# A recurrence with a feed-forward on one core: SyncE's issues in the list, later moves and stores, kept banks, later feed-forward ranks

## The chip, the core and the metric

The kernel runs on one core of a Trainium2 chip. The metric is the device time of one execution in microseconds; several runs are taken and their median is given. A core has five engines, each with its own instruction queue that is worked off in order: TensorE (PE, with its weight loads PEld), VectorE (DVE), ScalarE (ACT), GpSimd (POOL) and SyncE (SP). They wait for each other by semaphores. Transfers are issued by SyncE and by GpSimd here and are carried by 16 DMA engines. TensorE writes into PSUM, which has eight banks.

## The reference

For 4 batches with 8 heads, 768 time steps and a head size of 40, a state of 40 x 40 per head is carried through time. Its outputs, gathered to 3072 tokens of 320, go through a feed-forward with squared ReLU:

```python
for t in range(S):                         # S = 768, per batch and head
    y[t]  = rt @ state
    Sa    = state @ at
    state = state * wt[None, :] - outer(Sa, bt) + outer(vt, kt)
x = y as (3072, 320)
h = x @ w_in                               # 320 x 2048
g = maximum(h, 0) ** 2
out = g @ w_out                            # 2048 x 320
```

## The kernel before

**The work.** Time is cut into 6 chunks (c) of 128 steps. A chunk has 4 input batches of 8 heads, so there are 24 units m = 4 c + batch, and each unit has two steps of 4 heads: 48 steps st = 2 m and 2 m + 1. A unit has

- six loads `("L", m, key)` of 160 KB for W, K, B, A, V, R (L244, issued on SyncE). Each of the six has a ring of four buffers, so a load of unit m can start only when unit m - 4 has been read;
- its preparation: logarithm and running sum of W (L257, L263), exponentials (L268), products KB (L279), casts on GpSimd (L285, L290), and transposes (L294) with their copies out of PSUM.

Each step is then a chain through PE, ACT and DVE: `ca` (L394), masked copies `CN` (L402), `P`, `corr1`, `corr2` (L417, L426), `tb` (L463), `ex` (L482), `EVX` (L487), `kbm` (L498), and at its end the outputs `YS` (L511) and the state `UZ` (L515). Four steps later in the list than `ca`, these close the step. From step 12 on, `ca` of one step and `ex` of the step three before are merged into one piece of PE work that takes four PSUM banks at once.

**The feed-forward.** Four steps (half a chunk, h = 0 to 11) give 256 tokens. Two of the eight heads lie on rows where the matmul cannot use them, so four small SBUF-to-SBUF transfers `("mv", h, x)` (L620, SyncE) move them first. Then come eight pieces `hp` (L630, six matmuls each into one bank), ReLU `hs` on ACT (L636), the square `Gt` on GpSimd or DVE (L641); then for two token blocks `op` (L658, sixteen matmuls in two parts), the copy `osb` (L662, ring of three) and the store `st` (L667, SyncE). Banks held by the feed-forward are capped at four, those of the preparation at three.

**The weights.** `w_in` comes as ten transfers into WIN[0..2], `w_out` as one into WOUT. GpSimd issues them (L596, L602), and the transfer makes bf16 of them.

**The order.** All of it is first collected as operations (`op(name, engine, rank, cost, lat, needs, bufs, fn)`): `cost` is how long the engine is taken, `lat` when the result is there, both in us, and the rank is about the step at which the operation is due. `listed()` then plays the engines forward. For each engine it looks at the first 60 open operations in the order of rank, works out by `beginning()` when each could start (engine free, needs ended, buffers and banks free), takes those within 0.06 us of the earliest, and of these the one with the lowest rank. The operations are emitted in that order. So the plan decides the order in each queue, and the chip keeps that order, whatever the real durations are: an operation whose input comes later than the plan thought holds up all that is behind it on its engine.

In the plan before, loads are on an engine of their own, "DQ", that stands for the DMA engines (0.97 us each). Moves and stores are on "SP" at 0.1 and 0.3 us. On the chip, loads, moves and stores are issued by SyncE's one queue, in the order of their planned starts. The weights take a time on "DQ" first (`WINq`, `WOUTq`), and the real issue on GpSimd is planned behind that.

Of the kernel before, what the change touches and what calls it, by code (L numbers as in the profile page):

```python
# [18 lines left out]
def kernel(  # L19
# [12 lines left out]
    nc = tc.nc  # L32

    NB, NHH, T, D = r.shape
    L = 128
# [11 lines left out]
    NH = 2 * NCH  # L47
# [68 lines left out]
    def act(n, more=0.0):  # L116
        return 0.093 + 0.00083 * n + more, 0.186 + 0.00083 * n

    def pe(n):
        return n, n + 0.165  # L120
# [20 lines left out]
    WIN = [gl.tile([128, DFF], BF16, name=f"WIN{g}") for g in range(PB - 1)]  # L141
    WOUT = gl.tile([128, NJ, DM], BF16, name="WOUT")
# [75 lines left out]
    for m in range(NBC):  # L218
        o = Batch()
# [18 lines left out]
    def add_load(m, key, rank):  # L238
        o = bt[m]
        c, bb = divmod(m, NB)  # L240

        def go():
            t_ = sb(o.nat[key], [128, NHH, D], FP32)
            nc.sync.dma_start(  # L244
                out=t_[:],
                in_=nat_srcs[key][bb, :, c * L:(c + 1) * L, :].rearrange("h t e -> t h e"))
        op(("L", m, key), "DQ", rank, 0.97, 3.0, [], [o.nat[key]], go)

    def add_prep(m):
        o = bt[m]  # L250
# [317 lines left out]
    def add_energy(hc):  # L568
        st0 = hc * (NQ // 2)
        c, q = divmod(st0, NQ)  # L570
        for x, (src, at) in enumerate(((Mcb[c], AM), (Ccb[c], AC))):
            jmb[hc, x] = buf("jm")

            def jm(x=x, src=src, at=at):
# [11 lines left out]
    MOVED = [(s, 64 * x + D, 2 * NG + s, (64 - D) * x, n)  # L586
             for s in range(2) for x, n in enumerate((64 - D, 2 * D - 64))]

    def add_weights():
        for g in range(NG):  # L590
            def go(g=g):
                if g == 2:
                    nc.vector.memset(WIN[2][:], 0.0)
                for p, row, h, e0, n in PLACE + MOVED:
                    if p == g:
                        nc.gpsimd.dma_start(out=WIN[p][row:row + n, :],  # L596
                                            in_=moe_w_in[h * D + e0:h * D + e0 + n, :])
            op(("WINq", g), "DQ", g - 4.0, 2.8, 2.8, [], [], lambda: None)
            op(("WIN", g), "POOL", g - 4.0, 0.3, 1.0, [("WINq", g)], [], go)

        def go():
            nc.gpsimd.dma_start(out=WOUT[:], in_=moe_w_out.rearrange("(j p) f -> p j f", p=128))  # L602
        op(("WOUTq",), "DQ", -1.5, 8.3, 8.3, [], [], lambda: None)
        op(("WOUT",), "POOL", -1.5, 0.5, 1.0, [("WOUTq",)], [], go)

    Gtb = [buf("Gt") for _ in range(NH)]

    def add_ff(h):
        c, hf = divmod(h, 2)
        st0 = c * NQ + hf * (NQ // 2)  # L610
        done = [("YS", st0 + i) for i in range(NQ // 2)]
        X_ = YSb[c]

        def by_pair():
            return X_.tile[:].rearrange("e (b p) t -> e p b t", b=NB)[:, :, HB * hf:HB * hf + HB, :]

        for x, (p, row, hh, e0, n) in enumerate(MOVED):
            def gather(p=p, row=row, hh=hh, e0=e0, n=n):
                src = 64 * (hh % 2) + e0
                nc.sync.dma_start(out=by_pair()[row:row + n, p], in_=by_pair()[src:src + n, hh // 2])  # L620
            op(("mv", h, x), "SP", st0 + 7.3 + 0.01 * x, 0.1, 2.0, done, [X_], gather)
        for jj in range(NJ // 2):
            hpb, hsb = buf("bank", "ff"), buf("hs")

            def ff_in(jj=jj, hpb=hpb):
                hp = hpb.tile[:].rearrange("p (u a b) -> p u a b", u=2, a=HB)
                for u in range(2):
                    j = 2 * jj + u
                    for g in range(NG):
                        nc.tensor.matmul(out=hp[:, u], lhsT=WIN[g][0:ROWS[g], j * 128:(j + 1) * 128],  # L630
                                         rhs=by_pair()[0:ROWS[g], g],
                                         start=(g == 0 and u == 0), stop=(g == NG - 1),
                                         skip_group_check=True)

            def relu(hpb=hpb, hsb=hsb):
                nc.scalar.activation(out=sb(hsb, [128, 512], BF16)[:], in_=hpb.tile[:],  # L636
                                     func=ACTF.Relu)

            def square(jj=jj, hsb=hsb, eng=None):
                t_ = sb(Gtb[h], [128, NJ, HB, L], BF16)  # L640
                eng.tensor_tensor(out=t_[:, 2 * jj:2 * jj + 2].rearrange("p j a b -> p (j a b)"),  # L641
                                  in0=hsb.tile[:], in1=hsb.tile[:], op=ALU.mult)

            rank = st0 + 8.0 + 0.45 * jj
            on = "POOL" if jj % 4 and h < NH - 1 else "DVE"
            op(("hp", h, jj), "PE", rank, *pe(0.654),
               [("mv", h, x) for x in range(len(MOVED))] + [("WIN", g) for g in range(NG)],
               [X_, hpb], ff_in, "F")
            op(("hs", h, jj), "ACT", rank + 0.3, *act(500), [("hp", h, jj)], [hpb, hsb], relu)
            op(("Gt", h, jj), on, rank + 0.6, *((0.99, 1.05) if on == "POOL" else (0.34, 0.45)),  # L650
               [("hs", h, jj)], [hsb, Gtb[h]],
               lambda f=square, on=on: f(eng=nc.gpsimd if on == "POOL" else nc.vector))
        for b_ in range(HB):
            opb, osbb = buf("bank", "ff"), buf("osb")

            def ff_out(part_, b_=b_, opb=opb):
                for j in range(part_ * NJ // 2, (part_ + 1) * NJ // 2):
                    nc.tensor.matmul(out=opb.tile[:, 0:DM], lhsT=Gtb[h].tile[:, j, b_, :],  # L658
                                     rhs=WOUT[:, j, :], start=(j == 0), stop=(j == NJ - 1))

            def copy_out(opb=opb, osbb=osbb):
                nc.scalar.activation(out=sb(osbb, [128, DM], FP32)[:], in_=opb.tile[:, 0:DM],  # L662
                                     func=ACTF.Copy)

            def store(b_=b_, osbb=osbb):
                tok = (HB * hf + b_) * T + c * L
                nc.sync.dma_start(out=out[tok:tok + L, :], in_=osbb.tile[:])  # L667

            for p in range(2):
                op(("op", h, b_, p), "PE", st0 + 10.8 + 1.8 * b_ + 0.3 * p, *pe(1.085),  # L670
                   [("Gt", h, 4 * p + i) for i in range(4)] + [("WOUT",)]
                   + ([("op", h, b_, 0)] if p else []),
                   [Gtb[h], opb], lambda p=p, f=ff_out: f(p), "F")
            op(("osb", h, b_), "ACT", st0 + 11.5 + 1.8 * b_, *act(302), [("op", h, b_, 1)],
               [opb, osbb], copy_out)
            op(("st", h, b_), "SP", st0 + 11.6 + 1.8 * b_, 0.3, 2.0, [("osb", h, b_)], [osbb], store)

    for m in range(NBC):
        add_prep(m)
# [19 lines left out]
    def add_guard():  # L699
# [6 lines left out]
        def judge():  # L706
# [21 lines left out]
    CROSS = {("PE", "ACT"): 0.05, ("PE", "DVE"): 0.05, ("ACT", "PE"): 0.11, ("DVE", "PE"): 0.11,  # L728
             ("ACT", "DVE"): 0.06, ("DVE", "ACT"): 0.06, ("POOL", "PE"): 0.11, ("SP", "PE"): 0.1}
    SWITCH, SLACK = 0.095, 0.06  # L730
    BIAS = {"FR": 0.3, "FC": 0.6, "CR": 0.3}
    START = {"PE": 4.0, "ACT": 2.2, "DVE": 4.0, "POOL": 5.2, "SP": 0.9, "DQ": 0.9}

    def listed():
        free = dict(START)
# [11 lines left out]
        out_ = []  # L747
        seen = set()

        def beginning(o, e):  # L750
            t = free[e]
            for nm in o.needs:
                d = ops[alias.get(nm, nm)]
                if d.end is None:
                    return None
                t = max(t, d.end + (CROSS.get((d.eng, e), 0.17 if e == "POOL" else 0.08)
                                    if d.eng != e else 0.0))
            new = 0
            for b_ in o.bufs:
                if b_.slot is not None:  # L760
                    continue
                if b_.ring == "bank":
                    new += 1
                    if b_.kind and held.get(b_.kind, 0) + 1 > CAP[b_.kind]:
                        return None
                else:
                    n = RING[b_.ring if b_.ring in RING else "N"]
                    if heads[b_.ring] != b_.n:
                        return None
                    if b_.n >= n:  # L770
                        old = rings[b_.ring][b_.n - n]
                        if old.left:
                            return None
                        t = max(t, old.end + 0.1)
            if new:
                spare = sorted(freed[i] for i in range(NBANK) if i not in taken)
                if len(spare) < new:
                    return None
                t = max(t, spare[new - 1] + 0.1)
            return t  # L780

        while any(todo.values()):
            best = None
            for e, row in todo.items():
                cand = []
                for o in row[:60]:
                    t = beginning(o, e)
                    if t is not None:
                        cand.append((t, o))
                if not cand:  # L790
# [153 lines left out]
```

## Time and profile before

| | us |
|---|---|
| median of 3 runs | 336.72 (335.22 to 338.42) |
| the profiled execution | 337.33 |
| its span, first to last instruction | 335.6 |
| mean granted TensorE clock | 0.92 |

The profile is of one execution. Busy times count instructions that compute; register, semaphore and DMA-issuing instructions are not counted, except in rows named SPq. A row of a wait names the waiting line, then what released it. Matmuls are pipelined and their ends are modelled, so that a busy PE need not be PE at its peak. Line numbers are those of the kernel before.

### The profile page before, as it was taken

How to read it: one execution, taken by the hardware profiler on the slowest of the kernel's cores; microseconds unless marked ns; L12 is line 12 of the kernel's file. 1: busy time of each engine (PE TensorE's matmuls, PEld its weight loads, DVE VectorE, ACT ScalarE, POOL GpSimd, SP SyncE). 2: the span in 40 equal slices, each digit the busy share in tenths (PEclk: the TensorE clock that was granted, in tenths of full speed). 3: DMA queues.
4: the chain of work that ended last, by engine and by line, in shares of the span. 5: the costliest groups of instructions: out<-in, count | busy, mean ns of one | idle time of the engine just before them, and what ended most of it. 6: DMA issues, size and time to landing. Idle time of an engine off the chain costs nothing.

```text
span 335.6 us, 9943 instructions
## 1 busy us (share of the span) xinstructions
PE 286.5 (85%) x3852; PEld 221.8 (66%) x3852; DVE 228.9 (68%) x523; ACT 203.7 (61%) x531; POOL 205.0 (61%) x350
## 2 busy tenths in 40 slices
PE   6798675578999599899699699899899898998894
PEld 4565454357778377687488587688687776776562
DVE  6579947046888669697478668697688688684330
ACT  4655444158896476776477477777687675656241
POOL 8658527157998569297378468396685682555300
PEclk9559959599999879999899979999999999799978
DMA  8996296439999698699725744633000001001011
GB/s 137 176 157 121 36 168 92 66 66 163 191 161 176 124 190 136 129 178 177 136 52 88 144 76 81 123 61 62 26 2 25 24 2 38 10 2 46 5 44 48
DMA packets 158472, 31.37 MB, mean 93 GB/s; under 512 B 152976, under 2 KB 158096, under 8 KB 158416
## 3 DMA queue, kind: packets, MB, share of 16 engines
q1 hardware_dynamic: 155808, 28.03, 46.5%
q0 software_dynamic: 2608, 2.62, 5.1%
q8 instruction: 32, 0.52, 0.7%
q14 instruction: 24, 0.20, 0.2%
HBM read 28.84 MB, written 3.93 MB: 98 GB/s over the span
## 4 chain that ended last, share of the span: by engine, by line
PE 51%; DMA 15%; DVE 14%; SPq 7%; POOL 4%; issue 4%; ACT 4%; DVEq 0%; POOLq 0%; ACTq 0%
PE bank L630 18%; PE bank L658 10%; DMA YS<-YS 7%; SPq L620 6%; PE bank L294 6%; DVE EVX L487 4%; PE bank L498 4%; DVE CN L402 3%; DMA WOUT<-in_moe_w_out_dram 3%; PE bank L263 3%; PE bank L394 2%; DMA NW<-in_w_dram 2%; PE bank L426 2%; DMA NA<-in_a_dram 2%; POOL KB L279 2%
## 5 line engine op out<-in xcount | busy, mean ns | idle before, releaser
L630 PE MATMUL bank<-YS,WIN 120*128 120x256 bf16 (+1 forms) x576 | 86.4, 294 | 24.7 <-DMA YS<-YS 24.1
L641 POOL TENSOR_TENSOR Gt<-hs 128x512 bf16<-128x512 bf16 x66 | 68.5, 1041 | 32.3 <-ACT hs L636 32.0
L636 ACT ACTIVATE hs<-bank 128x512 bf16<-128x512 f32 x96 | 57.0, 598 | 50.7 <-PE bank L630 44.8
L630 PEld LDWEIGHTS <-WIN 120*128 120x128 bf16 (+1 forms) x576 | 56.1, 104 | 43.4 <-DMA YS<-YS 24.7
L487 DVE TENSOR_TENSOR EVX<-bank,MEX 128x512 bf16<-128x512 f32 x96 | 65.1, 684 | 14.0 <-PE bank L482 12.8
L402 DVE TENSOR_TENSOR CN<-bank,MCN 128x512 bf16<-128x512 f32 x96 | 64.6, 682 | 4.2 <-PE bank L394 3.7
L658 PE MATMUL bank<-WOUT,Gt 128*128 128x320 bf16 x384 | 60.1, 302 | 7.1 <-DMA WOUT<-in_moe_w_out_dram 7.1
L658 PEld LDWEIGHTS <-Gt 128*128 128x128 bf16 x384 | 35.6, 98 | 20.1 <-issue 7.1
L451 ACT ACTIVATE jk<-CN 128x512 bf16<-128x512 bf16 x48 | 30.1, 628 | 16.5 <-DVE CN L402 16.3
L443 POOL TENSOR_TENSOR x<-Mc,c 128x160 f32<-128x160 bf16 x48 | 23.5, 490 | 26.5 <-DVE c L439 26.1
L515 DVE TENSOR_TENSOR UZ<-bank,GT 64x80 bf16<-64x80 f32 x80 | 18.8, 236 | 25.6 <-PE bank L505 13.4
L279 POOL TENSOR_TENSOR KB<-NK,GI 128x320 bf16<-128x320 f32 (+1 forms) x25 | 21.2, 850 | 24.1 <-ACT GI L268 23.8
L641 DVE TENSOR_TENSOR Gt<-hs 128x512 bf16<-128x512 bf16 x30 | 15.1, 503 | 23.5 <-ACT hs L636 23.3
L342 ACT ACTIVATE KBT<-bank 128x1024 bf16<-128x1024 bf16 (+1 forms) x25 | 24.7, 987 | 9.7 <-PE bank L294 7.8
L447 POOL TENSOR_TENSOR Cc<-x,EVX 128x160 bf16<-128x160 f32 x48 | 23.8, 496 | 9.9 <-ACT EVX L536 8.5
L426 PEld LDWEIGHTS <-CN 128*128 128x128 bf16 x384 | 21.2, 99 | 8.9 <-issue 4.0
L439 DVE TENSOR_TENSOR c<-bank,Mc 128x160 bf16<-128x160 f32 x48 | 15.3, 319 | 16.9 <-PE bank L426 15.1
L498 PE MATMUL bank<-EVX,KB 128*64 128x168 bf16 x384 | 24.7, 248 | 1.7 <-DVE EVX L487 1.5
L474 DVE COPY TB<-bank 128x512 bf16<-128x512 bf16 (+1 forms) x48 | 18.9, 395 | 4.6 <-PE bank L469 3.8
L263 PE MATMUL bank<-lnW,UTI 128*128 128x320 f32 x48 | 21.0, 523 | 1.2 <-ACT lnW L257 0.9
L511 DVE TENSOR_TENSOR YS<-bank,GT 128x256 bf16<-128x256 f32 x48 | 20.2, 421 | 2.5 <-PE bank L505 2.1
L268 ACT ACTIVATE GI<-bank 128x320 f32<-128x320 f32 x24 | 10.5, 436 | 17.6 <-PE bank L263 17.6
(82 smaller groups left out, 545.3 us busy)
## 6 DMA issues: line engine op xcount, KB each, us to landing
NW<-in_w_dram SPq DMA_DIRECT2D x24, 160.0 KB
NK<-in_k_dram SPq DMA_DIRECT2D x24, 160.0 KB
NB<-in_b_dram SPq DMA_DIRECT2D x24, 160.0 KB
NA<-in_a_dram SPq DMA_DIRECT2D x24, 160.0 KB
NV<-in_v_dram SPq DMA_DIRECT2D x24, 160.0 KB
NR<-in_r_dram SPq DMA_DIRECT2D x24, 160.0 KB
out_dram<-osb SPq DMA_DIRECT2D x24, 160.0 KB
WOUT<-in_moe_w_out_dram POOLq DMA_DIRECT2D x1, 1280.0 KB, 10.2
```

Source lines behind the costliest of these rows:

```text
L263: nc.tensor.matmul(out=csb.tile[:, 0:NHH * D], lhsT=UTI[:], rhs=o.lnW.tile[:], start=True, stop=True)
L279: eng.tensor_tensor(out=o.KB.tile[:, u, h, 0:D], in0=o.nat[key].tile[:, h], in1=o.GI.tile[:, h], op=ALU.mult)
L342: nc.scalar.activation(out=t_[:, :, j0:j0 + n], func=ACTF.Copy, in_=bank(b2)[:, 0:2 * n * L].rearrange("p (u j t) -> p u j t", u=2, t=L))
L402: nc.vector.tensor_tensor(out=t_[:, :, s], in0=quads(ca[s]), in1=MCN[:], op=ALU.mult)
L426: nc.tensor.matmul(out=P[:, 2 * i + s], lhsT=CN[:, i, s, 1, :], rhs=X[:, 2 * i + s], start=False, stop=last, skip_group_check=True)
L451: nc.scalar.activation(out=t_[:], in_=CN_.tile[:, :, :, 1, :], func=ACTF.Square, accum_out=ACC[:, AN + st:AN + st + 1])
L487: nc.vector.tensor_tensor(out=EVX[:, :, s, 0:2 * LV].rearrange("p i (u x) -> p i u x", u=2)[:, :, :, 0:L], in0=quads(ex[s]), op=ALU.mult, ...
L498: nc.tensor.matmul(out=uy()[half(s), i, :], lhsT=o.KB.tile[:, u, 2 * (j0 + i) + s, :], rhs=EVX[:, i, s, LV * u:LV * u + LV], start=(i == 0 ...
L630: nc.tensor.matmul(out=hp[:, u], lhsT=WIN[g][0:ROWS[g], j * 128:(j + 1) * 128], rhs=by_pair()[0:ROWS[g], g], start=(g == 0 and u == 0), st ...
L636: nc.scalar.activation(out=sb(hsb, [128, 512], BF16)[:], in_=hpb.tile[:], func=ACTF.Relu)
L641: eng.tensor_tensor(out=t_[:, 2 * jj:2 * jj + 2].rearrange("p j a b -> p (j a b)"), in0=hsb.tile[:], in1=hsb.tile[:], op=ALU.mult)
L658: nc.tensor.matmul(out=opb.tile[:, 0:DM], lhsT=Gtb[h].tile[:, j, b_, :], rhs=WOUT[:, j, :], start=(j == 0), stop=(j == NJ - 1))
```

## The change

1. **SyncE's queue.** Loads move from "DQ" to "SP" in the plan; "DQ" is gone. A move costs 0.82 us there instead of 0.1, a store 0.45 instead of 0.3.
2. **Moves and stores.** For all halves but the last two, `beginning()` adds 2.5 us to what a move waits for, and 6.0 us to what a store waits for. Their ranks drop, from 7.3 to -9.0 and from 11.6 to 4.6 (after the half's first step), so that they go first once they may.
3. **The weights.** The issues on GpSimd get ranks from 0.5 to 2.5 and wait for casts of units 1, 2, 2 and 3. The transfer's time follows the issue, in shares on "SP" that emit nothing. The clearing of WIN[2] becomes an operation of its own on DVE with the lowest rank.
4. **Banks.** An operation that could start within 0.3 us but finds too few banks reserves its number; operations ranked behind it may take a bank only beyond these.
5. **Feed-forward.** The ranks of `hp` (with `hs` and `Gt`) rise by 4 steps, those of `op` and `osb` by 5.

```diff
-        op(("L", m, key), "DQ", rank, 0.97, 3.0, [], [o.nat[key]], go)
+        op(("L", m, key), "SP", rank, 0.97, 2.9, [], [o.nat[key]], go)
...
+    GATE = [("cast", 1, "A", 0), ("cast", 2, "A", 0), ("cast", 2, "X", 0), ("cast", 3, "A", 0)]
+
+    def share(name, issue, n, each):
+        for i in range(n):
+            last = i == n - 1
+            op(name if last else (*name, i), "SP", -5.0, each, each + 2.0 * last,
+               [(*name, i - 1) if i else issue], [], lambda: None)
+
...
-                if g == 2:
-                    nc.vector.memset(WIN[2][:], 0.0)
...
-            op(("WINq", g), "DQ", g - 4.0, 2.8, 2.8, [], [], lambda: None)
-            op(("WIN", g), "POOL", g - 4.0, 0.3, 1.0, [("WINq", g)], [], go)
+            n = sum(x[0] == g for x in PLACE + MOVED)
+            op(("WINi", g), "POOL", 0.5 + 0.5 * g, 0.52 * n, 0.52 * n, [("WIN2",), GATE[g]], [], go)
+            share(("WIN", g), ("WINi", g), n, 0.7)
...
-        op(("WOUTq",), "DQ", -1.5, 8.3, 8.3, [], [], lambda: None)
-        op(("WOUT",), "POOL", -1.5, 0.5, 1.0, [("WOUTq",)], [], go)
+        op(("WOUTi",), "POOL", 2.5, 1.23, 1.3, [GATE[3]], [], go)
+        share(("WOUT",), ("WOUTi",), 9, 0.92)
+        op(("WIN2",), "DVE", -5.0, 1.0, 1.1, [], [], lambda: nc.vector.memset(WIN[2][:], 0.0))
...
-            op(("mv", h, x), "SP", st0 + 7.3 + 0.01 * x, 0.1, 2.0, done, [X_], gather)
+            op(("mv", h, x), "SP", st0 - 9.0 + 0.01 * x, 0.82, 2.0, done, [X_], gather)
...
-            rank = st0 + 8.0 + 0.45 * jj
+            rank = st0 + 12.0 + 0.45 * jj
...
-                op(("op", h, b_, p), "PE", st0 + 10.8 + 1.8 * b_ + 0.3 * p, *pe(1.085),
+                op(("op", h, b_, p), "PE", st0 + 15.8 + 1.8 * b_ + 0.3 * p, *pe(1.085),
...
-            op(("osb", h, b_), "ACT", st0 + 11.5 + 1.8 * b_, *act(302), [("op", h, b_, 1)],
+            op(("osb", h, b_), "ACT", st0 + 16.5 + 1.8 * b_, *act(302), [("op", h, b_, 1)],
...
-            op(("st", h, b_), "SP", st0 + 11.6 + 1.8 * b_, 0.3, 2.0, [("osb", h, b_)], [osbb], store)
+            op(("st", h, b_), "SP", st0 + 4.6 + 1.8 * b_, 0.45, 2.0, [("osb", h, b_)], [osbb], store)
...
+    LATE = {"mv": 2.5, "st": 6.0}
...
-    START = {"PE": 4.0, "ACT": 2.2, "DVE": 4.0, "POOL": 5.2, "SP": 0.9, "DQ": 0.9}
+    START = {"PE": 4.0, "ACT": 2.2, "DVE": 4.0, "POOL": 5.2, "SP": 0.9}
...
-        def beginning(o, e):
+        def beginning(o, e, kept):
...
-                                    if d.eng != e else 0.0))
+                                    if d.eng != e else 0.0)
+                        + (LATE[o.name[0]] if o.name[0] in LATE and o.name[1] < NH - 2 else 0.0))
...
-                if len(spare) < new:
+                if len(spare) < new + kept[0]:
+                    if t < free[e] + 0.3:
+                        kept[0] += new
                     return None
...
-                cand = []
+                cand, kept = [], [0]
...
-                    t = beginning(o, e)
+                    t = beginning(o, e, kept)
```

## The prediction

> **What bounds the kernel now.** I read the page first, then the waits of all engines, the windows of 10 us, and then the queue of SyncE and the neighbourhood of the stalls in the timeline. The page says which engine is the fullest:
>
> ```profile
> span 335.6 us, 9943 instructions
> ...
> PE 286.5 (85%) x3852; PEld 221.8 (66%) x3852; DVE 228.9 (68%) x523; ACT 203.7 (61%) x531; POOL 205.0 (61%) x350
> ...
> q1 hardware_dynamic: 155808, 28.03, 46.5%
> q0 software_dynamic: 2608, 2.62, 5.1%
> ...
> L636 ACT ACTIVATE hs<-bank 128x512 bf16<-128x512 f32 x96 | 57.0, 598 | 50.7 <-PE bank L630 44.8
> ```
>
> PE is idle for 335.6 - 286.5 = 49.1 us. The waits (engine, line, releaser: us in total, times, longest) tell for what:
>
> ```profile
> PE bank L630 <- DMA YS<-YS: 24.1, 19, 2.8
> ...
> PE bank L658 <- DMA WOUT<-in_moe_w_out_dram: 7.1, 1, 7.1
> ```
>
> 24.1 + 7.1 = 31.2 us of the 49.1 are two kinds of DMA. The rest, 17.9 us, is scattered. The windows (start:end, length, busy us and instructions of PE, PEld, DVE, ACT, POOL, then granted PE clock, DMA share, GB/s) show what stands between the stalls, and what a stall leaves behind:
>
> ```profile
> 40.00:50.00 10.00, 6.52 (x56) 4.63 (x57) 5.35 (x12) 4.08 (x12) 2.70 (x5) 0.66 0.98 164
> ...
> 60.00:70.00 10.00, 7.59 (x56) 4.88 (x55) 1.27 (x5) 2.54 (x8) 3.73 (x7) 0.66 0.21 31
> ...
> 80.00:90.00 10.00, 10.00 (x159) 8.20 (x158) 7.30 (x17) 9.12 (x29) 8.89 (x16) 1.00 0.94 175
> ...
> 110.00:120.00 10.00, 6.05 (x51) 3.98 (x46) 5.06 (x12) 4.66 (x15) 4.52 (x9) 0.73 0.77 132
> 120.00:130.00 10.00, 10.00 (x161) 8.07 (x161) 8.46 (x19) 7.55 (x19) 8.54 (x12) 0.92 1.16 165
> ...
> 160.00:170.00 10.00, 6.69 (x73) 4.74 (x73) 3.41 (x9) 4.34 (x14) 3.50 (x5) 0.83 0.60 116
> ...
> 190.00:200.00 10.00, 8.32 (x111) 7.21 (x113) 5.42 (x13) 5.55 (x16) 5.79 (x8) 0.83 0.64 117
> ...
> 280.00:290.00 10.00, 8.52 (x108) 6.66 (x107) 6.61 (x14) 5.51 (x12) 2.44 (x4) 0.83 0.08 23
> ...
> 320.00:336.00 16.00, 10.96 (x79) 8.13 (x77) 3.41 (x8) 5.45 (x10) 0.00 (x0) 0.82 0.15 48
> ```
>
> Where nothing stalls (80 to 90), PE is busy throughout and the granted clock is 1.00. Every window with a stall has the other engines down too, and a clock of 0.66 to 0.83. So PE bounds the kernel, and what can be won is its stalls and the slow clock in and behind them. Better packing of the good windows has nothing left to win.
>
> **Part 1: SyncE's queue, and the moves.** Each half of a chunk (12 in all) ends in four small moves (YS to YS, L620) before its feed-forward may start. The SyncE timeline and then PE's show one of them; in both, the columns are start, length, instruction and, in brackets, the idle time before it:
>
> ```profile
> 111.19 4.00 SPq L620 DMA_DIRECT2D YS<-YS  x4
> ```
> ```profile
> 114.84 0.39 PE L630 MATMUL bank<-YS,WIN 120*128 120x256 bf16 x1 [2.60 <-DMA YS<-YS]
> 116.36 3.81 PE L630 MATMUL bank<-YS,WIN 120*128 120x256 bf16 x17 [1.13 <-DMA YS<-YS]
> 119.96 0.34 PE L411 MATMUL bank<-UZ,AT 128*128 128x80 bf16 x2
> ```
>
> And the chain of waits has the landing of the last move, here and at the last half:
>
> ```profile
> 114.57 1.75 DMA YS<-YS
> ...
> 317.94 1.76 DMA YS<-YS
> ```
>
> From the first issue at 111.19 to the landing at 114.57 + 1.75 = 116.32 pass 5.1 us. The old list gives a move 0.1 us of SyncE and 2.0 us to land, so four are done after 0.3 + 2.0 = 2.3 us: 2.8 us too early here. PE's order is fixed by that list, so the feed-forward matmuls stand at PE's head too early and everything behind them waits, although it is ready: the recurrent matmuls at 119.96 follow without a wait once the feed-forward has run. 24.1 us over 12 halves is 2.0 us a half, which agrees with this gap. The new list gives 3 x 0.82 + 2.0 = 4.5 us, and for ten of the twelve halves 2.5 us more (LATE): 7.0 us, more than the 5.1 seen. What covers the wait is the recurrence of the next steps and, with the feed-forward ranked 4 to 5 steps later, pieces of the half before. The last two halves have no LATE, but their 4.5 us is close to the 5.1, and leftovers of the half before cover them. I leave 5 of the 24.1 us for halves whose moves come later than listed: **-19 us**. If the cover is not there, all 24 stay.
>
> The stores (L667) get the same treatment, LATE 6.0. No engine waits for a store except through the three osb buffers, two per half, so 6 us out of a half's 335.6 / 12 = 28 us cost nothing. What they hold up is the loads behind them, as do the moves. SyncE's own waits:
>
> ```profile
> SPq L620 <- DVE YS L511: 47.7, 5, 20.3
> SPq L667 <- ACT Mc L529: 39.0, 6, 18.1
> ...
> SPq L244 <- POOL KB L279: 19.9, 16, 4.6
> ...
> SPq L244 <- POOL RV L290: 13.1, 6, 5.7
> ```
>
> The longest, 20.3 us, is a move waiting at SyncE's head for its YS while the loads behind it stand. With moves later among the loads these waits shrink. On PE they are worth little by themselves, for PE has few waits on loads (they lie in the 17.9 us); I book nothing. The new danger is the reverse: a load ahead of a move can itself wait up to 5.7 us for its buffer (last row), and the move with it. That is a rival below.
>
> **Part 2: the weights.** GpSimd's timeline, then the chain:
>
> ```profile
> 33.37 0.45 POOL L290 CAST GA<-NA 128x320 bf16<-128x320 f32 x1
> ...
> 38.77 1.10 POOL L596 DMA_DIRECT2D WIN<-in_moe_w_in_dram  x2 [2.48 <-DVE WIN L593]
> ...
> 52.02 1.23 POOL L602 DMA_DIRECT2D WOUT<-in_moe_w_out_dram  x1
> ```
> ```profile
> 52.02 10.21 DMA WOUT<-in_moe_w_out_dram
> ```
>
> PE's timeline at that place, and the first of the windows:
>
> ```profile
> 62.27 2.29 PE L658 MATMUL bank<-WOUT,Gt 128*128 128x320 bf16 x8 [7.10 <-DMA WOUT<-in_moe_w_out_dram]
> ```
> ```profile
> 0.00:10.00 10.00, 6.46 (x56) 4.80 (x57) 6.83 (x21) 4.87 (x11) 8.45 (x36) 0.94 0.86 146
> ```
>
> The old list puts the issue of WOUT after the time that it thinks the transfer takes, so the real transfer begins when it should have ended; PE waits for it up to 62.2. Now the issue hangs on the cast of A of batch 3, which ran at 33.4 us: issue near 34, 18 us earlier, landing near 34 + 10.2 = 44 us, or 54 if sharing doubles the transfer. PE's stall began at 62.27 - 7.10 = 55.2. **-7 us**. The pieces of WIN hang on earlier casts, and the clearing of WIN[2] goes to VectorE's start, which takes GpSimd's 2.48 us wait out; VectorE is busy 6.83 of the first 10 us. The share operations issue nothing; they only push listed loads later, and the real queue keeps their order. Against it: the weights (5.1% of 335.6 = 17 us of all DMA engines) now compete with the loads of batches 2 to 5, each 46.5% x 335.6 / 144 = 1.1 us (moves and stores in it, so a little less). Batch 3 could come some 7 us later; before, its cast at 33.37 waited for nothing. **+2 us**, between 0 and 7.
>
> The Trainium skill, DMA: Bandwidth & Descriptors, section Queues, rings and completion order, says that each DMA engine takes turns between the queues that have work, so WOUT would not go ahead of the loads as the list assumes. By that an estimate for its landing is 54 us instead of 44, and the sum would be up to 2 us worse; no row here has WOUT beside loads at their full rate.
>
> **Part 3: the clock.** Busy time times what the clock lacked, in the windows above behind stalls: 6.52 x 0.34 + 7.59 x 0.34 + 6.05 x 0.27 + 10.0 x 0.08 + 6.69 x 0.17 + 8.32 x 0.17 + 8.52 x 0.17 + 10.96 x 0.18 = 13 us. With four fifths of the stalls gone I take 70% of it: **-9 us**.
>
> **Part 4: banks kept, and later feed-forward.** A merged step of the recurrence needs four of the eight banks at once; now, while it lacks only banks, nothing ranked behind it may take one. No wait of this kind is in the trace. It can win nothing in windows that are full; at the other end PE idles in each of the 48 steps until one feed-forward bank is read out, 0.60 us by the L636 row: 29 us. A gain is bounded by the 17.9 us scattered idle time, of which I would give it half at most. I take **+5 us**, near nothing, because a bank comes free in that time only where feed-forward holds one just then. Later feed-forward leaves more of it to the end; it is PE work either way, and there is PE time only once for it: nothing, as long as PE stays full.
>
> **The sum**, against the profiled execution's 337.3 us: -19 - 7 - 9 + 2 + 5 = -28, so 309. The median of the runs, 336.7, is 0.6 lower: **308 us**.
>
> **Rivals.** *The kept banks starve PE* (slower). It acts at each step; the price is idle time per step times 48. Without its +5 the sum is 303, so it cancels the gain at 34 / 48 = 0.7 us a step, a little over one L636; with two in a row part of the time, 1.0 us, the time is 303 + 48 = 351. For it: ScalarE is 61% busy and reads a feed-forward bank only in its turn. Against it: two or three feed-forward matmul groups per step, capped at four banks, and the recurrence has operations that need no new bank. *Moves caught behind loads* (no gain from part 1): if half of the halves lose 5.7 - 2 = 3.7 us and keep their clock loss, 6 x 3.7 = 22 us come back: 308 + 22 + 4 = 334. For it are the 16 and 6 waits of loads for GpSimd; against it, that they were counted in a queue that was itself disturbed by stalls. *The change does not act*, since list and chip drift apart anyway: then PE's 24.1 us stay, only WOUT's 7 and its clock loss of 2.6 go, 327; I count this into the second.
>
> **Chances.** Forecast 0.68. Moves caught or no effect 0.15, centred on 333 and reaching across the bound. Kept banks starving PE 0.17. A measurement here can tell about 1% from no change, 333.4 to 340.1: faster 0.68 + 0.08 = 0.76, same 0.07, slower 0.17. The range: at the low end nothing of part 4's cost and half of the scattered idle time gone too, 308 - 5 - 9 = 294, and 1 us less in part 2: 293. At the high end it takes in the second rival, up to 340; the slower rival stays out.
>
> **What would show it.** Right: PE's wait for YS below 6 us and for WOUT none; WOUT issued near 34 us; mean clock from 0.92 to 0.95 or more; few windows with PE below 8 us between 40 and 300; SyncE's wait at L620 far below 47.7 us. Wrong: new waits of PE on ScalarE's L636 or VectorE's evictions (kept banks); L630 still waiting for YS with loads just ahead of the moves on SyncE; or VectorE as the full engine with a long stretch of feed-forward alone at the end, which would mean that feed-forward was put off too far.

## The result, and the profile after

The changed kernel takes 294.88 us (median of 4 runs, 294.21 to 297.0) against 336.81 us before: a ratio of 0.8766 with a 95% interval of 0.8705 to 0.8827. The forecast was 308 us, so the direction and the range held, but the time is only 2 us above the range's low end of 293, and the gain of 42 us is half as large again as the 28 us of the sum. Here and below, ratios are taken from undisturbed executions alone, so some differ a little from the quotient of the medians.

The page of the changed kernel, first lines and the chain by engine:

```profile
span 292.5 us, 9938 instructions
...
PE 272.7 (93%) x3852; PEld 216.1 (74%) x3852; DVE 227.7 (78%) x523; ACT 201.2 (69%) x531; POOL 202.9 (69%) x350
...
PE 72%; DVE 9%; POOL 7%; ACT 6%; issue 2%; DMA 1%; POOLq 0%; DVEq 0%; ACTq 0%
```

PE is idle for 292.5 - 272.7 = 19.8 us instead of 49.1, and it is busy for 272.7 us instead of 286.5 with the same 3852 matmuls. 29.3 + 13.8 = 43.1 us, the whole difference of the spans. In the chain that ended last, DMA and SyncE's queue had 22% before (the row below); now DMA has 1%, and SyncE's queue is not in it.

```profile
PE 51%; DMA 15%; DVE 14%; SPq 7%; POOL 4%; issue 4%; ACT 4%; DVEq 0%; POOLq 0%; ACTq 0%
```

The groups of instructions by line show both parts in one row (count, busy us, mean ns, then the idle time before it and what ended it). First comes the feed-forward's first row in the kernel before, where L638 was L630 and L666 was L658, then two rows of the changed kernel:

```profile
L630 PE MATMUL bank<-YS,WIN 120*128 120x256 bf16 (+1 forms) x576 | 86.4, 294 | 24.7 <-DMA YS<-YS 24.1
```

```profile
L638 PE MATMUL bank<-YS,WIN 120*128 120x256 bf16 (+1 forms) x576 | 77.0, 273 | 0.0
...
L666 PE MATMUL bank<-WOUT,Gt 128*128 128x320 bf16 x384 | 60.2, 301 | 0.3 <-ACT GA L268 0.2
```

Before, L658 had 7.1 us of waiting for WOUT. Both waits are gone, and the same 576 matmuls are 9.4 us shorter. The clock records of the two traces say why: before, 88 of the 576 started while the granted clock was 0.50 and took 412 ns on average, the others 273 ns at 1.00; in the changed kernel all 576 start at 1.00. PE's longest waits are now these:

```profile
PE bank L417 <- DVE CN L402: 2.5, 5, 0.9
...
PE bank L498 <- DVE EVX L487: 1.6, 3, 1.0
...
PE bank L294 <- POOL KB L279: 1.4, 1, 1.4
```

None of them is on a DMA. The first two are inside the recurrence, the third is in the preparation (transposes that wait for GpSimd's products). The windows show where the rest of the idle time lies:

```profile
30.00:40.00 10.00, 8.22 (x126) 6.02 (x125) 9.54 (x24) 4.71 (x15) 5.66 (x11) 0.83 0.87 126
40.00:50.00 10.00, 8.91 (x113) 6.47 (x114) 9.08 (x24) 6.52 (x17) 5.37 (x8) 0.83 0.87 136
50.00:60.00 10.00, 7.96 (x82) 5.94 (x80) 4.43 (x8) 4.39 (x9) 6.26 (x10) 0.83 0.58 101
60.00:70.00 10.00, 10.00 (x144) 7.99 (x143) 6.47 (x14) 8.36 (x27) 7.50 (x13) 1.00 1.00 178
...
110.00:120.00 10.00, 9.97 (x160) 8.26 (x158) 9.89 (x23) 9.23 (x26) 9.26 (x15) 1.00 0.83 142
...
280.00:292.50 12.50, 6.56 (x52) 4.80 (x50) 1.50 (x4) 3.11 (x6) 0.00 (x0) 0.92 0.14 46
```

From 90 us to 280 us PE is busy for 9.6 us or more of each 10, at a granted clock of 1.00 (the row from 110 stands for them; before, it had 6.05 us and 0.73). The idle time that is left lies ahead of 60 us, between 80 and 90, and in the last 6 us, when the last copy and store run out. The mean clock went from 0.920 to 0.967.

The weights, on GpSimd's timeline of the changed kernel:

```profile
14.64 2.26 POOL L602 DMA_DIRECT2D WIN<-in_moe_w_in_dram  x4
21.53 2.09 POOL L602 DMA_DIRECT2D WIN<-in_moe_w_in_dram  x4
26.72 1.07 POOL L602 DMA_DIRECT2D WIN<-in_moe_w_in_dram  x2
34.54 1.23 POOL L609 DMA_DIRECT2D WOUT<-in_moe_w_out_dram  x1
```

WOUT is issued at 34.54 us; 34 was forecast.

### The profile page after: what moved, and what is told of

Same layout as the page of the kernel before. It is cut to its first block, busy times and chain, and to the rows that moved or that the text cites. A ratio compares the mean times of both kernels' runs of the same rounds, so it can differ in the third digit from the quotient of the medians.

```text
span 292.5 us, 9938 instructions
## 1 busy us (share of the span) xinstructions
PE 272.7 (93%) x3852; PEld 216.1 (74%) x3852; DVE 227.7 (78%) x523; ACT 201.2 (69%) x531; POOL 202.9 (69%) x350
## 4 chain that ended last, share of the span: by engine, by line
PE 72%; DVE 9%; POOL 7%; ACT 6%; issue 2%; DMA 1%; POOLq 0%; DVEq 0%; ACTq 0%
PE bank L638 20%; PE bank L666 17%; PE bank L294 9%; PE bank L498 5%; PE bank L263 4%; PE bank L394 4%; PE bank L426 3%; PE bank L482 3%; DVE EVX L487 3%; DVE CN L402 3%; PE bank L505 2%; POOL KB L279 2%; PE bank L463 2%; ACT jk L451 2%; PE bank L469 1%
## 5 line engine op out<-in xcount | busy, mean ns | idle before, releaser
L638 PE MATMUL bank<-YS,WIN 120*128 120x256 bf16 (+1 forms) x576 | 77.0, 273 | 0.0
L644 ACT ACTIVATE hs<-bank 128x512 bf16<-128x512 f32 x96 | 57.5, 601 | 22.5 <-PE bank L638 20.0
L666 PE MATMUL bank<-WOUT,Gt 128*128 128x320 bf16 x384 | 60.2, 301 | 0.3 <-ACT GA L268 0.2
L638 PEld LDWEIGHTS <-WIN 120*128 120x128 bf16 (+1 forms) x576 | 51.8, 97 | 9.9 <-issue 0.6
L666 PEld LDWEIGHTS <-Gt 128*128 128x128 bf16 x384 | 36.0, 98 | 13.5 <-issue 0.5
L649 DVE TENSOR_TENSOR Gt<-hs 128x512 bf16<-128x512 bf16 x30 | 14.2, 473 | 19.6 <-ACT hs L644 19.3
L498 PE MATMUL bank<-EVX,KB 128*64 128x168 bf16 x384 | 23.7, 243 | 1.6 <-DVE EVX L487 1.6
L394 PE MATMUL bank<-AT,KBT 64*128 64x128 bf16 x384 | 19.6, 226 | 1.2 <-DVE AT L336 1.1
L263 PE MATMUL bank<-lnW,UTI 128*128 128x320 f32 x48 | 19.6, 491 | 0.8 <-DVE EVX L487 0.4
## 6 DMA issues: line engine op xcount, KB each, us to landing
WOUT<-in_moe_w_out_dram POOLq DMA_DIRECT2D x1, 1280.0 KB, 10.6
```

The lines of the kernel that those rows point to most:

```text
L263: nc.tensor.matmul(out=csb.tile[:, 0:NHH * D], lhsT=UTI[:], rhs=o.lnW.tile[:], start=True, stop=True)
L394: nc.tensor.matmul(out=quads(ca[s])[:, i, u, :], lhsT=o.KBT.tile[half(s), u, j0 + i, :], rhs=o.AT.tile[half(s), j0 + i, :], start=(i == 0 ...
L498: nc.tensor.matmul(out=uy()[half(s), i, :], lhsT=o.KB.tile[:, u, 2 * (j0 + i) + s, :], rhs=EVX[:, i, s, LV * u:LV * u + LV], start=(i == 0 ...
```

## The experiments

In this section and in the expectations, parts are numbered as in the list of the change. My theory was that the moves' listing (parts 1 and 2) takes the wait for YS away, the weights' listing takes the wait for WOUT away, and kept banks and ranks are worth little. The rival was that the later ranks give the cover. Each part was tried alone on the kernel before, and each was undone alone in the changed kernel; then single numbers were changed. Ratios are to the kernel before, run beside it on the same chip.

| run | what | us | ratio (95%) |
|---|---|---|---|
| e1_sync | before + SyncE's issues, moves and stores | 313.1 | 0.932 (0.923 to 0.940) |
| e2_weights | before + weights | 329.2 | 0.981 (0.972 to 0.990) |
| e3_ranks | before + later ranks | 304.8 | 0.908 (0.901 to 0.915) |
| e4_banks | before + kept banks | 333.6 | 0.990 (0.985 to 0.996) |
| u1_sync | changed, SyncE's part undone | 306.5 | 0.915 (0.905 to 0.926) |
| u2_weights | changed, weights undone | 301.4 | 0.900 (0.891 to 0.910) |
| u3_ranks | changed, ranks undone | 300.7 | 0.897 (0.888 to 0.907) |
| u4_banks | changed, banks undone | 294.4 | 0.879 (0.869 to 0.889) |
| m1_landing | before + a move's listed landing | 316.1 | 0.943 (0.926 to 0.959) |
| m2_moves_old | changed, moves listed as before | 305.4 | 0.911 (0.896 to 0.926) |
| m3_store_early | changed, stores not later | 295.5 | 0.886 (0.871 to 0.902) |
| x_late6 | changed, moves 6.0 us later | 294.3 | 0.882 (0.868 to 0.897) |

**One number: when a move lands.** The sharpest test of the theory changes nothing but the listed landing.

```diff
-            op(("mv", h, x), "SP", st0 + 7.3 + 0.01 * x, 0.1, 2.0, done, [X_], gather)
+            op(("mv", h, x), "SP", st0 + 7.3 + 0.01 * x, 0.1, 4.8, done, [X_], gather)
```

> The kernel before with one number changed: a move's listed landing 4.8 us instead of 2.0, so that four are listed to land after 5.1 us, what the trace shows. Costs on SyncE, ranks, loads, stores, weights and banks are as before. If the wait for YS is nothing but the list's error about this landing, it falls from 24.1 us to below 6 and the time by 20 us or more, to 316 or less. If the loads behind the moves or the order of SyncE's queue make it, it stays above 12 us.

316.1 us, some 19 us less than the kernel before by the ratio, at the edge of the 316 that was expected. The waits of that run:

```profile
PE bank L658 <- DMA WOUT<-in_moe_w_out_dram: 6.3, 1, 6.3
...
PE bank L630 <- DMA YS<-YS: 3.3, 4, 1.6
```

The wait for YS fell from 24.1 to 3.3 us, and WOUT's stayed, as it should. So the stall was the list's error about one duration: the costs on SyncE, the loads' entries and the ranks are those of before.

**SyncE's part alone**: loads on "SP", costs, ranks and LATE of moves and stores, with the weights still on "DQ".

```diff
-        op(("L", m, key), "DQ", rank, 0.97, 3.0, [], [o.nat[key]], go)
+        op(("L", m, key), "SP", rank, 0.97, 2.9, [], [o.nat[key]], go)
...
-            op(("mv", h, x), "SP", st0 + 7.3 + 0.01 * x, 0.1, 2.0, done, [X_], gather)
+            op(("mv", h, x), "SP", st0 - 9.0 + 0.01 * x, 0.82, 2.0, done, [X_], gather)
...
-            op(("st", h, b_), "SP", st0 + 11.6 + 1.8 * b_, 0.3, 2.0, [("osb", h, b_)], [osbb], store)
+            op(("st", h, b_), "SP", st0 + 4.6 + 1.8 * b_, 0.45, 2.0, [("osb", h, b_)], [osbb], store)
...
+    LATE = {"mv": 2.5, "st": 6.0}
...
```

> The kernel before with parts 1 and 2 of the change alone: SyncE's issues counted, moves and stores later. If the costs of the moves are what takes PE's wait for YS away (my theory), this alone brings that wait from 24.1 us to below 6 and the time to about 337 - 20 - 6 (clock) = 311 us; WOUT's 7 us wait stays. If the later feed-forward ranks give the cover (the rival), moves that are listed rightly still find no other work for PE, the wait turns into idle time on other rows, and the time stays above 325.

313.1 us, and PE's waits in that run are

```profile
PE bank L630 <- DMA YS<-YS: 3.6, 2, 1.9
PE bank L263 <- ACT lnW L257: 7.1, 2, 6.9
```

The theory's numbers came for the moves. The second row is new, and WOUT's wait, which was expected to stay, is gone. Both are the experiment's own doing: with "DQ" to themselves, the weights are listed (and on the chip issued) much earlier, WOUT at 22.6 us instead of 52.0, and the loads pay for it (the last section has the rows). The size of this part is therefore better read from the runs that undo parts.

**The ranks alone.**

```diff
-            rank = st0 + 8.0 + 0.45 * jj
+            rank = st0 + 12.0 + 0.45 * jj
...
-                op(("op", h, b_, p), "PE", st0 + 10.8 + 1.8 * b_ + 0.3 * p, *pe(1.085),
+                op(("op", h, b_, p), "PE", st0 + 15.8 + 1.8 * b_ + 0.3 * p, *pe(1.085),
...
-            op(("osb", h, b_), "ACT", st0 + 11.5 + 1.8 * b_, *act(302), [("op", h, b_, 1)],
+            op(("osb", h, b_), "ACT", st0 + 16.5 + 1.8 * b_, *act(302), [("op", h, b_, 1)],
```

> The kernel before with part 5 alone: feed-forward ranked 4 to 5 steps later. Theory: the list still believes that a move lands after 2.3 us, so PE's wait for YS stays at 18 us or more wherever feed-forward is the only thing listed there, and the time stays within 10 us of 337. Rival: the wait falls below 8 us and the time to 315 or less, because ranks alone put other work ahead.

304.8 us: the rival's side, by a wide margin, and the largest effect of any single part. The wait for YS in that run:

```profile
PE bank L630 <- DMA YS<-YS: 3.0, 2, 2.8
```

The list still believes that moves land after 2.3 us, and it does not matter: PE has recurrence of a lower rank to do, and the feed-forward is taken up much later than its data. PE's wait for WOUT (7.1 us before) is gone as well, although GpSimd still issues it at 52.0 us and it lands at 62.5. The second feed-forward product, which needs it, is ranked five steps later, and PE has other work up to its first matmul, which follows without idle time but with nothing to spare:

```profile
62.13 0.40 PE L394 MATMUL bank<-AT,KBT 64*128 64x128 bf16 x8
62.52 1.25 PE L658 MATMUL bank<-WOUT,Gt 128*128 128x320 bf16 x8
```

So the 31 us of the ranks hold both stalls, that for the moves and that for WOUT. How much later the feed-forward comes can be read off the timelines. The table has, for the twelve halves, the us from the end of the issue of the last move to the half's third feed-forward matmul (the first two are the ones that wait for the moves). 1.3 to 2.0 us is the landing itself: PE has waited for it. In the first half the landing is slower (3.6 us before).

```
before         3.6  1.3  1.4  1.3  2.0  1.9  1.3  1.3  1.4  1.3  1.3  1.4
e3_ranks       3.5  2.7  1.3  3.3 10.2  7.7 15.3 17.4 17.3 15.3  9.2  6.1
u3_ranks       5.1  4.5  3.3  4.3  4.6  3.7  3.0  5.0  4.1  3.8  2.1  1.3
changed        5.2  5.7  4.7  8.0 14.8 18.4 14.4 16.5 16.4 14.6  9.3  4.9
```

The ranks (e3) make room of 8 to 17 us from the fifth half to the tenth, when the recurrence has run ahead, and hardly any in the first four. The listing (u3: all of the change but the ranks) makes an even 3 to 5 us up to the tenth half, and next to none in the last two, where LATE does not apply. The changed kernel has both.

**Undone in the changed kernel: the ranks, then SyncE's part.** The ranks go back to 8.0, 10.8 and 11.5 (the diff above, reversed).

> The changed kernel with part 5 undone: feed-forward ranked as before. Theory: most of the gain stays, since the moves are listed rightly; 295 to 302 us. Rival (ranks give the cover): 310 us or more.

300.7 us: most of the gain stays, as the theory has it. SyncE's part undone is the diff of e1_sync reversed, with the loads and the weights' shares on "DQ":

```diff
...
-    LATE = {"mv": 2.5, "st": 6.0}
+    LATE = {}
...
-    START = {"PE": 4.0, "ACT": 2.2, "DVE": 4.0, "POOL": 5.2, "SP": 0.9}
+    START = {"PE": 4.0, "ACT": 2.2, "DVE": 4.0, "POOL": 5.2, "SP": 0.9, "DQ": 0.9}
```

> The changed kernel with parts 1 and 2 undone: loads on an engine of their own in the list, moves and stores at their old costs and ranks. Theory: PE's wait for YS comes back with 15 us or more, and the time is 294.9 + 20 = 315 us or more. Rival (the later ranks cover it): below 302.

306.5 us, between the two. PE's timeline and the windows of that run show where it loses:

```profile
38.97 0.27 PE L417 MATMUL bank<-EVX,CN 128*128 128x40 bf16 x4
44.17 0.37 PE L638 MATMUL bank<-YS,WIN 120*128 120x256 bf16 x1 [4.94 <-DMA YS<-YS]
```

```profile
40.00:50.00 10.00, 4.98 (x33) 3.56 (x34) 3.44 (x8) 3.10 (x12) 3.08 (x4) 0.67 1.01 156
60.00:70.00 10.00, 7.88 (x107) 5.60 (x106) 5.05 (x10) 6.58 (x19) 4.33 (x9) 1.00 0.72 120
120.00:140.00 20.00, 16.81 (x258) 13.68 (x256) 15.76 (x38) 12.04 (x32) 11.55 (x21) 0.91 0.91 150
```

The first half has no recurrence ahead of it and no earlier feed-forward, so the ranks cannot help: PE stands 4.9 us for the first moves. After that the wait for YS is 1.4 us in all. The windows from 60 and from 120 stall otherwise, on GpSimd's casts (1.6 us) and on ScalarE's reading of a bank (3.2 us). In this run SyncE stood 8.8 us before the second move, until 58.6 us, with loads behind it (5.1 us in the changed kernel); that the loads are the cause was not tried by itself.

With the weights in place, the four runs make a square: neither part 329.2 (e2, which has no kept banks either), SyncE's part 300.7, ranks 306.5, both 294.9. Alone they are worth 28.5 and 22.7 us, together 34.3: some 17 us are the same stall, which either one removes. The 17 is rough: the first of the four also lacks kept banks and lists the weights' shares on "DQ", and the medians come from different chips.

**Moves listed as before, loads still counted.**

```diff
-            op(("mv", h, x), "SP", st0 - 9.0 + 0.01 * x, 0.82, 2.0, done, [X_], gather)
+            op(("mv", h, x), "SP", st0 - 9.0 + 0.01 * x, 0.1, 2.0, done, [X_], gather)
...
-    LATE = {"mv": 2.5, "st": 6.0}
+    LATE = {"st": 6.0}
```

> The changed kernel with the moves listed as before (0.1 us on SyncE, no extra 2.5 us), loads and stores still counted, later ranks kept. If the later ranks cover the wait by themselves: no wait for YS above 4 us, and 295 to 298 us. If the moves' listing is what the 11.6 us of the run with SyncE's parts undone came from: 302 us or more, with moves waiting at SyncE's head in front of loads.

305.4 us. So most of what u1_sync lost came from the moves' listing (cost and extra time together); counting loads on "SP" is worth little without it.

**The weights, alone and undone.** Alone, the shares stand on "DQ"; undone, the old operations stand on "SP".

```diff
...
-            op(("WINq", g), "DQ", g - 4.0, 2.8, 2.8, [], [], lambda: None)
-            op(("WIN", g), "POOL", g - 4.0, 0.3, 1.0, [("WINq", g)], [], go)
+            op(("WINi", g), "POOL", 0.5 + 0.5 * g, 0.52 * n, 0.52 * n, [("WIN2",), GATE[g]], [], go)
+            share(("WIN", g), ("WINi", g), n, 0.7)
...
-        op(("WOUTq",), "DQ", -1.5, 8.3, 8.3, [], [], lambda: None)
-        op(("WOUT",), "POOL", -1.5, 0.5, 1.0, [("WOUTq",)], [], go)
+        op(("WOUTi",), "POOL", 2.5, 1.23, 1.3, [GATE[3]], [], go)
+        share(("WOUT",), ("WOUTi",), 9, 0.92)
...
```

> The kernel before with part 3 alone: weights issued behind the casts, their transfer listed behind the issue. Theory: PE's wait for WOUT (7.1 us) is gone and 2.6 us of slow clock with it, 327 us. The rival that stalls are only shifted: the wait for YS of the second half takes its place, 334 or more.

329.2 us, 6.7 us less than the kernel before beside it (335.97); the interval takes in 1.0 to 2.8%. The wait for WOUT is gone; the other stands as it was:

```profile
PE bank L638 <- DMA YS<-YS: 24.2, 17, 4.7
```

> The changed kernel with part 3 undone: the weights listed as a transfer first and an issue behind it, now on SP since DQ is gone. Theory: PE waits for WOUT again, some 7 us and 2 to 3 us of slow clock: 303 to 306 us. Rival (feed-forward is late enough not to notice): within 2 us of 294.9.

301.4 us, 6.5 us more than the changed kernel. Its cost is not a wait for WOUT, as I had written: PE waits for no DMA in that run. It lies in the early part, in which PE and its clock are both low:

```profile
30.00:40.00 10.00, 7.57 (x110) 5.46 (x109) 7.09 (x19) 5.69 (x17) 4.57 (x9) 0.67 0.23 43
40.00:50.00 10.00, 5.69 (x73) 3.97 (x74) 9.33 (x21) 3.98 (x12) 5.22 (x9) 0.67 0.74 120
```

The first feed-forward matmul starts at 53.5 us there, at 45.2 in the changed kernel, and until then PE runs only the recurrence and the preparation, with their waits. Two things differ that could make it so: the last of WIN is issued at 40.9 us instead of 27.3, and SyncE issues no load from 22.4 us to the first move at 39.0, where the changed kernel issues loads until 32.5. Which of them costs the 6.5 us was not tried.

**Kept banks, alone and undone.**

```diff
...
-                if len(spare) < new:
+                if len(spare) < new + kept[0]:
+                    if t < free[e] + 0.3:
+                        kept[0] += new
                     return None
...
```

> The kernel before with part 4 alone: banks kept for operations that wait. Theory: waits for YS and WOUT stay at 24 and 7 us, and the time changes by -5 to +5 us. The rival that kept banks starve PE: +15 us or more, with PE idle behind ScalarE's L636 or VectorE's evictions.

333.6 us, 2 to 3 us less than before, with the waits where they were (YS 21.4 us, WOUT 7.3).

> The changed kernel with part 4 undone: no banks kept. My prediction booked +5 us for kept banks, so this would be 290 us; if they cost nothing, 294.9 within 1%; if the recurrence needs them to run ahead, slower than 298.

294.4 us, the same as with them. In neither trace does PE wait for ScalarE's ReLU to read out a bank (L636, L644), which is where starving would show. Waits that could be for a bank are few and short: 1.8 us once in e4_banks (L630 behind `CN`), 0.2 to 0.4 us each in u4_banks. Kept banks are worth some 1% on the old list (0.5 to 1.5% by the interval) and nothing that can be told on the new one.

**Stores not later, and moves later still.**

```diff
-    LATE = {"mv": 2.5, "st": 6.0}
+    LATE = {"mv": 2.5}
```

> The changed kernel without the extra 6.0 us for stores. If stores cost nothing, as I predicted, 294.9 within 1%. If stores that wait at SyncE's head hold up loads that PE needs: 298 us or more.

295.5 us: stores cost nothing, although SyncE's own queue shows that they do wait at its head without the 6.0 us (first the run without them, then the changed kernel):

```profile
SPq L675 <- ACT osb L670: 60.2, 16, 10.7
```

```profile
SPq L675 <- ACT osb L670: 36.8, 8, 7.5
```

```diff
-    LATE = {"mv": 2.5, "st": 6.0}
+    LATE = {"mv": 6.0, "st": 6.0}
```

> The changed kernel with 6.0 us instead of 2.5 us of extra time for moves. In the changed kernel SyncE still stands 5 to 6 us before the first two moves while loads queue behind them, and PE has 2 us of idle time in each 10 us up to 60. If that is the cause, up to 5 us are won, 290 us; if the loads are bound by the DMA engines there or the later landing stalls PE, 295 or slower.

294.3 us, no gain that can be told. SyncE's timeline of that run has the first two moves where they were (37.0 and 50.1 us in the changed kernel):

```profile
37.50 3.31 SPq L628 DMA_DIRECT2D YS<-YS  x4
...
49.88 3.07 SPq L628 DMA_DIRECT2D YS<-YS  x4
```

Three more loads stand ahead of the second move than in the changed kernel (W, K, B of the next unit), and PE's idle time up to 60 us is about the same. So the loads behind the second move were not what holds PE there; what does stays open. No version beat the changed kernel by more than the runs scatter.

## Why the prediction was right, and where its sizes were off

**What bounds the kernel**: right. PE was the engine to fill, its stalls and the clock behind them were what could be won, and 43.1 us of span went from exactly these two, 29.3 of idle time and 13.8 of busy time.

**Part 1, the moves (-19)**: the mechanism was right and is shown by m1_landing, where one number of the list takes 20.8 of the 24.1 us away. The size was too small. I left 5 us for moves that come later than listed, and PE has no wait for YS left. In the changed kernel the moves start at most 0.2 us after their YS in eleven halves and 2.1 us after it in one, so the rival "moves caught behind loads" did not happen. One sign came only in part: I wanted SyncE's wait at L620 far below 47.7 us. That row (moves waiting for YS) fell to 23.6 us, all of SyncE's waits at moves together from 70.8 to 52.0 us, and the time came without it. What I booked at nothing, the place of the moves among the loads, the runs cannot separate from the first half's stall: together they are 11 us of u1_sync and m2_moves_old.

**Part 2, the weights (-7, +2)**: right when taken alone (e2). With the 2.6 us of clock that belong to it the three terms make -7.6 us; the two profiles differ by 8.5 us, 5.4 of idle time (-7 + 2 = -5 was booked) and 3.1 of busy time, and the medians by 6.7. In the changed kernel the issue came at 34.54, and the landing 10.6 us later, at 45.1 us: the undisturbed case of the two that I gave. The doubled transfer, by which the sum would have been 2 us worse, did not come, and little ran beside it: SyncE stood before the first move until 37 us, and its queue moved 0.24 MB while WOUT was on its way, against 1.08 MB in e1_sync. But the 7 us are not this part's alone: the ranks also take the wait for WOUT away (e3).

**Part 3, the clock (-9)**: too small, because I took 70% of 13 us. PE is busy for 13.8 us less. By the same product of busy time and missing clock, the windows behind 40 us have 8.91 x 0.17 + 7.96 x 0.17 + 6.56 x 0.08 = 3.4 us left, 9.7 less than 13. My product left out the first 40 us, which had 7.2 us of it before and have 4.2 now; there the clock scatters from run to run (0.50 between 10 and 20 us in u4_banks, 0.70 in the changed kernel), so that part is no sure gain. One reading was wrong: not every window with a stall has a slow clock. The one with most of the wait for WOUT had 1.00; the slow clock came in the window behind it:

```profile
50.00:60.00 10.00, 5.18 (x76) 3.67 (x74) 6.35 (x15) 3.99 (x9) 6.43 (x8) 1.00 0.76 105
```

**Part 4, banks and ranks (+5)**: the step that failed. Kept banks cost nothing that can be told (u4), so the rival of PE starved by them is out. And "later feed-forward: nothing" is wrong as an account of the ranks: alone they are worth 31 us (e3), more than any other part, because a feed-forward that comes 8 to 17 us behind its data needs no right listing of the moves, and because WOUT has landed when its second product is due. On top of all the rest they are worth 6 us (u3). In the sum this hardly showed, since I had given the same stalls to the listings of moves and weights, and named the delayed feed-forward as the cover of the moves. That the ranks could be booked at nothing without harm to the sum is in part luck: what they win alone was already booked to the listings.

The difference of 15 us between the sum (-28) and the spans (-43) is thus 5 us of stalls that I left standing, 5 us of clock, and 5 us of banks that cost nothing. The low end of the range was to be reached through half of the scattered idle time; that is not how it came about, for the idle time outside the two stalls went from 17.9 to 19.8 us.

## What to carry to other kernels

Where a planner fixes the order of in-order queues, compare its listed duration for each DMA with the trace, from the first issue to the last landing: here a queue's head that was due some 2 us too early in each half cost PE 24 us, and some of the clock after it. There are two remedies that do not add up: list the true duration, or rank the consumer so late that the error does not matter; the first also works at the start, where there is nothing to be late behind. Before booking parts of a change separately, ask which of them would remove the same idle time, and count that only once.

## What the runs showed of the hardware

Weights and loads do slow each other in e1_sync, but not evenly. WOUT was issued there at 22.6 us, beside 1.08 MB of SyncE's transfers, and landed after 14.3 us, against 10.2 us before, where SyncE's queue moved nothing meanwhile, and 10.6 us in the changed kernel, where it moved 0.24 MB. A doubling would have been 20 us. The loads paid more: one issue on SyncE took 5.14 us (the longest of a load before is 2.28), while the nineteen issues of loads after the landing took 0.6 to 2.0 us each. W of a unit came 7.5 us late for ScalarE, and so for PE (SyncE's timeline, then ScalarE's and PE's, of e1_sync):

```profile
25.30 5.14 SPq L244 DMA_DIRECT2D NK<-in_k_dram  x1
30.49 4.26 SPq L244 DMA_DIRECT2D NB<-in_b_dram  x1
```

```profile
37.17 0.47 ACT L257 ACTIVATE lnW<-NW 128x320 f32<-128x320 f32 x1 [7.46 <-DMA NW<-in_w_dram]
```

```profile
37.69 1.44 PE L263 MATMUL bank<-lnW,UTI 128*128 128x320 f32 x2 [6.88 <-ACT lnW L257]
```

The Trainium skill, DMA: Bandwidth & Descriptors, section Queues, rings and completion order, has each engine take turns between queues at packet granularity. The run agrees that both queues go on; the 14.3 us instead of 20 say that the turns did not halve this transfer, whose rows are 1280 bytes in memory, beside loads of 160-byte rows.
